# The start of a Fourier-mixing and dense-layer kernel: last filter product through SBUF, tables moved between engines, one set of PSUM pools, and stage 1 of the next batch a slot earlier

## Chip, cores, metric

One core of one Trainium2 chip. The metric is the device time of one execution in microseconds (us), all data in device memory at the start. Lower is better. The kernel is already tuned; its matrix engine has work 99% of the time.

## The reference

```python
X = np.fft.rfft(x, axis=1)                      # x: (8, 3008, 256)
y = np.fft.irfft(X * (filt_r + 1j*filt_i), n=3008, axis=1)
h = y.reshape(24064, 256) @ w_in                # 256 x 2048
g = 0.5 * h * (1 + erf(h / sqrt(2)))            # exact GELU
out = g @ w_out                                 # 2048 x 256, float32
```

## The kernel before

The transform of 3008 points is split as 47 x 64 and done with matmuls in four stages, each against a table of sines. Stage 2's result is multiplied by the filter F on VectorE. Batch 0 is transformed alone at the start, because the dense layers need it, and its intermediate results are turned with TensorE transposes. Batches 1 to 7 are transformed in between the dense matmuls, one piece per *slot*; a slot is one step of 128 hidden columns (`mm1`, 2 matmuls) and, from slot 16 on, one step of the second layer (`mm2`, 4 matmuls). Their intermediate results pass through DRAM (R1, R2). Matmuls write to PSUM, in *banks*; an *eviction* copies a bank to SBUF, the core's on-chip memory. `a_sb` holds the result of stage 1, `vt_sb` that of batch 0's third stage, `d_sb` its transposes and `y_sb` the finished transform. Warm-up matmuls are matmuls on a tile of ones whose result nobody reads.

The last product of batch 0 and its third stage:

```python
def c2(self, p):                       # stage 2 and filter product of batch 0
    w = self.st[0, "p", p] = self.pp.tile([128, 2, 512], BF16, tag="p12", name="p12")
    ps = self.bank("ps_c2", "w")
    ...                                # two matmuls into ps
    if p < 11:
        nc.vector.tensor_tensor(out=w, in0=ps..., in1=f..., op=ALU.mult)
        return
    w, ps = w.rearrange("p t (a b) -> p t a b", a=2), ps.rearrange("p (a b) -> p a b", a=2)
    for c in (slice(0, 128), slice(128, 256)):      # the last one in two pieces
        nc.vector.tensor_tensor(out=w[:, :, :, c], in0=ps[:, :, c]..., in1=f[:, :, :, c], op=ALU.mult)

# main program: products two ahead of the third stage, with warm-up matmuls between
for q in range(1, 7):
    ...
    if q < 6:
        m.c3(2 * q - 2)
        if q == 3:
            m.table_3(2)
            m.table_3_copy(2, True)
        else:
            m.warm_up(1)
    else:
        m.c3(10, 1)
        m.warm_up(1)
        m.c3(11, 1)
m.warm_up(2)
```

The last stages of batch 0, the change of PSUM pools, and the slots of batch 1:

```python
m.psum(wide, v=(4, 1), t=(4, 1))
for u in range(10):
    if u < 8:
        m.c3t(u)                                    # transposes, then d_sb by VectorE
    if u >= 2:
        m.c4(u - 2, (act, False if u > 7 else act)) # stage 4, then y_sb
wide.close()                                        # pools v and t end here
m.psum(ctx, h=(3, 1), o=(2, 1), f=(3, 1))           # pools of the dense layers
...
if b == 1:
    s1, n1, r1, s2, n2, r2, s4, n4 = 1, 4, 16, 26, 2.8, 61, 68, 0.72
```

So batch 1 has stage 1 in slots 1, 5, 9, 13, stage 2 from slot 26, stage 4 from slot 68.

```python
self.pa = pool("pa", 3)                             # three buffers of a_sb
...
def s1(self, b, c):                                 # c = 0..3
    a = self.pa.tile([128, 2, 4, 256], BF16, tag="a", name="a_sb")
    ps = [[self.bank("ps_s1", "h" if i == h == 0 else "f") for h in range(2)] for i in range(2)]
    ...                                             # 8 matmuls
    ...                                             # four evictions on VectorE, ps -> a
    for r in range(2):
        for h in range(2):
            nc.sync.dma_start(out=o[:, w:w + 4, :], in_=a[64 * r:64 * r + 48, h])   # R1 in DRAM
```

Stage 1 takes 8 matmuls and four evictions on VectorE in a slot; its four PSUM banks are one of three of `h`, shared with the dense layers, and all three of `f`. And there are four tiles of `a_sb` but only three buffers.

Of the kernel before, what the change touches and what calls it, by code (L numbers as in the profile page):

```python
# [29 lines left out]
class _Mix:  # L30
# [63 lines left out]
    def dup_filters(self, eng, k0, k):  # L94
        for k in range(k0, k0 + k, 2):
            o, i = (self.F[r:r + 64, :, k:k + 2, :].rearrange("p t a b -> p t (a b)") for r in (64, 0))
            eng.tensor_copy(out=o, in_=i)  # L97

# [26 lines left out]
    def table_1(self, g):  # L125

        nc, ts = self.nc, self.nc.vector.tensor_scalar
        col = lambda name: g.tile([128, 1], FP32, name=name)
        off = g.tile([128, 2, K1], FP32, name="off")
        nc.vector.memset(off[:, 0, :], 0.25)  # L130
        nc.vector.memset(off[:, 1, :], 0.5)
        h, n1, hs, hc = col("h"), col("n1"), col("hs"), col("hc")
        ts(out=h, in0=self.p, scalar1=float(NA), scalar2=None, op0=ALU.is_ge)
        nc.vector.scalar_tensor_tensor(out=n1, in0=h, scalar=-float(NA), in1=self.p, op0=ALU.mult, op1=ALU.add)
        ts(out=hs, in0=h, scalar1=2.0 * PI, scalar2=None, op0=ALU.mult)
        ts(out=n1, in0=n1, scalar1=1.0 / NA, scalar2=None, op0=ALU.mult)
        ts(out=hc, in0=h, scalar1=-2.0 * PI, scalar2=2.0 * PI, op0=ALU.mult, op1=ALU.add)
        self.turn_signs(g)
        self.weights_4(g)
        w, r = g.tile([128, 2, K1], FP32, name="w1"), g.tile([128, 2, K1], FP32, name="r1")  # L140
        nc.vector.scalar_tensor_tensor(out=w, in0=self.k48, scalar=n1, in1=off, op0=ALU.mult, op1=ALU.add)
        ts(out=r, in0=w, scalar1=RND, scalar2=-RND, op0=ALU.add, op1=ALU.add)
        nc.vector.tensor_tensor(out=w, in0=w, in1=r, op=ALU.subtract)
        for q, s in enumerate((hc, hs)):
            nc.scalar.activation(out=self.T1[:, 48 * q:48 * q + 48], in_=w[0:2 * NA].rearrange("p a b -> p (a b)"),
                                 func=AF.Sin, scale=s[0:2 * NA])
# [16 lines left out]
    def table_2_angle(self, g, h):  # L163


        v = self.nc.vector
        ts = v.tensor_scalar
        w = self.gen[:, 0]
        if h == 0:
            col = lambda name: g.tile([128, 1], FP32, name=name)  # L170
            jn = g.tile([128, NB], FP32, name="jn")
            ts(out=jn, in0=self.jj, scalar1=self.n2, scalar2=self.ri, op0=ALU.mult, op1=ALU.add)
            n6, self.n12 = col("n6"), col("n12")
            ts(out=n6, in0=self.n2, scalar1=6.0, scalar2=None, op0=ALU.mult)
            ts(out=self.n12, in0=self.n2, scalar1=12.0, scalar2=None, op0=ALU.mult)
            v.scalar_tensor_tensor(out=w[:, 0:6], in0=self.kk.unsqueeze(2).to_broadcast([128, 6, NB]), scalar=self.n2,
                                   in1=jn.unsqueeze(1).to_broadcast([128, 6, NB]), op0=ALU.mult, op1=ALU.add)
            ts(out=w[:, 6:12], in0=w[:, 0:6], scalar1=n6, scalar2=None, op0=ALU.add)
        else:
            ts(out=w[:, 12:24], in0=w[:, 0:12], scalar1=self.n12, scalar2=None, op0=ALU.add)  # L180
        k = slice(12 * h, 12 * h + 12)
        ts(out=self.gen[:, 1, k].bitcast(I32), in0=w[:, k].bitcast(I32), scalar1=15, scalar2=None,
           op0=ALU.logical_shift_left)

    def turn_signs(self, g):

        ts = self.nc.vector.tensor_scalar
        q, b = (g.tile([128, 1], FP32, name=n) for n in ("q64", "b32"))
        self.turn = [g.tile([128, 1], FP32, name=n) for n in ("turn_r", "turn_i")]
        ts(out=q, in0=self.p, scalar1=64.0, scalar2=-64.0, op0=ALU.is_ge, op1=ALU.mult)  # L190
        self.nc.vector.tensor_tensor(out=q, in0=self.p, in1=q, op=ALU.add)
        ts(out=b, in0=q, scalar1=32.0, scalar2=2.0, op0=ALU.is_ge, op1=ALU.mult)
        ts(out=self.turn[0], in0=b, scalar1=1.0, scalar2=-1.0, op0=ALU.mult, op1=ALU.add)
        ts(out=self.turn[1], in0=b, scalar1=-1.0, scalar2=1.0, op0=ALU.mult, op1=ALU.add)

# [23 lines left out]

    def weights_4(self, g):  # L220

        ts = self.nc.vector.tensor_scalar
        q, self.wt, self.wtc = (g.tile([128, 1], FP32, name=n) for n in ("q48", "wt", "wtc"))
        ts(out=q, in0=self.p, scalar1=48.0, scalar2=-48.0, op0=ALU.is_ge, op1=ALU.mult)
        self.nc.vector.tensor_tensor(out=q, in0=self.p, in1=q, op=ALU.add)
        ts(out=self.wt, in0=q, scalar1=2.0, scalar2=1.0, op0=ALU.is_ge, op1=ALU.add)
        ts(out=self.wtc, in0=self.p, scalar1=4.0, scalar2=1.0, op0=ALU.is_ge, op1=ALU.add)


# [13 lines left out]

    def table_3_copy(self, q, turn):

        v = self.t3.rearrange("p (k n r) -> p k r n", k=8, r=2)
        self._evac(self.T3[:, 8 * q:8 * q + 8], v, "act")
        if turn:
            for r in range(2):
                self._evac(self.T3i[:, 8 * q:8 * q + 8, r, :], v[:, :, 1 - r, :], "act", self.turn[r])  # L250

    def table_3_turn(self, q):

        k = slice(8 * q, 8 * q + 8)
        for r in range(2):
            self.nc.vector.tensor_scalar(out=self.T3i[:, k, r, :], in0=self.T3[:, k, 1 - r, :],
                                         scalar1=self.turn[r], scalar2=None, op0=ALU.mult)

# [142 lines left out]
    def c2(self, p):  # L401
# [9 lines left out]
        if p < 11:  # L411
            nc.vector.tensor_tensor(out=w, in0=ps.unsqueeze(1).to_broadcast([128, 2, 512]),
                                    in1=f.rearrange("p t a b -> p t (a b)"), op=ALU.mult)
            return
        w, ps = w.rearrange("p t (a b) -> p t a b", a=2), ps.rearrange("p (a b) -> p a b", a=2)
        for c in (slice(0, 128), slice(128, 256)):
# [3 lines left out]
    def c3(self, p, np=2):  # L420
# [11 lines left out]
        for half in range(2):  # L432
            v = self.vt[:, half, 0:96, :].rearrange("c a b -> c (a b)").rearrange("c (n k) -> c n k", n=HB)
            self._evac(v[:, :, 8 * p:8 * p + 8 * np], ps[half][:, 0:256 * np].rearrange("c (k n) -> c n k", n=HB),
                       False if p == 11 and half else "act")

    def c3t(self, u):
# [3 lines left out]
        d = self.st[0, "d", u // 2]  # L441
        ps = self.bank("ps_c3t", "t", BF16)
        for i in (0, 2, 4, 6, 1, 3, 5, 7):
# [6 lines left out]
    def c4(self, u, eng):  # L450
# [5 lines left out]
        for half in range(2):  # L456
            ps = self.bank("ps_c4", "v")
            for i in range(4):
# [69 lines left out]
def kernel(  # L528
# [25 lines left out]
    for sgn, lo, base in ((1, 0, 0), (-1, 32, m.S - NA)):  # L554
# [6 lines left out]
    nc.vector.memset(m.ones, 1.0)  # L561
    m.warm_up(10)
    m.table_1(g)
    m.table_2_rows(g)
    m.T1c = g.tile([2 * NA, 96], BF16, name="T1c")
    nc.vector.tensor_copy(out=m.T1c.rearrange("p (k h r) -> p k h r", h=2, r=2),
                          in_=m.T1.rearrange("p (h r k) -> p k h r", h=2, r=2))
    m.gen = m.py.tile([128, 2, K1, NB], FP32, tag="y", name="gen")
    m.table_2_angle(g, 0)
    m.unit_matrices(g, cols)  # L570
    m.T3i = m.pg.tile([128, K1, 2, NB], BF16, tag="g", name="T3i")
    m.vt = m.pg.tile([128, 2, 97, 32], BF16, tag="g", name="vt_sb")
    for k, n in ((0, 4), (4, 8), (12, 12)):
# [8 lines left out]
    for u in range(16):  # L582
# [7 lines left out]
        if u == 7:  # L590
            m.table_2_sin(1)
            m.table_3(0)
            m.table_3_copy(0, False)
            m.warm_up(2)
        if u == 11:
            m.table_2_swap(1)
            m.table_4(m.T4c, m.T1q, m.wtc, "n", False)
            m.table_3_turn(0)
            m.warm_up(1)
    m.table_3(1)  # L600
    m.table_3_copy(1, False)
    m.dup_filters(nc.vector, 0, 4)
    m.warm_up(1)
    m.c1t(0, (False, False))
    m.c1t(1, (act,))
    m.c2(0)
    m.table_3_turn(1)
    m.warm_up(1)
    m.c2(1)
    m.c1t(2, (act,))  # L610
    m.warm_up(2)
    for q in range(1, 7):
        if q < 6:
            m.c2(2 * q)
            if q + 2 < 6:
                m.c1t(q + 2, (act,))
            if q != 3:
                m.warm_up(2)
            m.c2(2 * q + 1)
        if q < 6:  # L620
            m.c3(2 * q - 2)
            if q == 3:
                m.table_3(2)
                m.table_3_copy(2, True)
            else:
                m.warm_up(1)
        else:
# [8 lines left out]
    m.load_w_out(0)  # L636
    m.load_w_out(8)

    warm = g.tile([128, 1], FP32, name="warm")
    nc.scalar.activation(out=warm, in_=m.p, func=AF.Gelu)  # L640
    wide.close()
    wide = ctx.enter_context(ExitStack())
    m.psum(wide, v=(4, 1), t=(4, 1))
    for u in range(10):
        if u < 8:
            m.c3t(u)
        if u >= 2:
            m.c4(u - 2, (act, False if u > 7 else act))
    wide.close()
    m.psum(ctx, h=(3, 1), o=(2, 1), f=(3, 1))  # L650

# [9 lines left out]
    for b in range(1, B):  # L661
        hi = first(b)
        if b == 1:
            s1, n1, r1, s2, n2, r2, s4, n4 = 1, 4, 16, 26, 2.8, 61, 68, 0.72
        else:
# [54 lines left out]
```

## Time and profile before

| | before |
|---|---|
| time, median of 6 runs | 772.76 us (772.1 to 775.15) |
| span of the profiled run | 770.6 us |
| TensorE busy | 763.5 us (99%) |
| first transposes of batch 0's third-stage result (`c3t`) | 31.05 us |
| first dense matmul | 38.76 us |
| first matmul of the second dense layer (slot 16) | 49.13 us |

From about 49 us on TensorE has work without gaps, so the time is decided by when that rhythm is reached. The main lines for this are in the prediction below. VectorE's evictions of stage 1 and the dense matmuls (columns of a timeline: start, busy us, engine, line, operation, output <- inputs, shape, count, and in brackets the idle time before and what ended it):

```profile
39.78 4.88 DVE L271 CAST a_sb<-ps_s 128x512 bf16<-128x512 f32 x8 [1.18 <-PE ps_s L296]
44.95 4.88 DVE L271 CAST a_sb<-ps_s 128x512 bf16<-128x512 f32 x8 [0.29 <-PE ps_s L296]
...
47.83 1.47 PE L482 MATMUL ps_h<-y_sb,w_in_sb 128*128 128x512 bf16 x6
49.13 0.60 PE L509 MATMUL ps_o<-w_out_sb,g_sb 128*128 128x256 bf16 x4
```

Sixteen evictions of 0.61 us run in two groups of eight; the only waits are for the matmuls.

### The profile page before, as it was taken

The numbers are of one execution on the slowest core, as the hardware profiler recorded it, in microseconds if no ns is written. First come the engines' busy times: TensorE is split into PE (matmuls) and PEld (weight loads), VectorE is DVE, ScalarE is ACT, GpSimd is POOL, SyncE is SP. The second block draws the span as 40 slices with busy tenths as digits, with TensorE's granted clock in tenths as the row PEclk, the third lists the DMA queues.
The fourth block names the chain that finished last, engine by engine and source line by source line (L and its number), as shares of the span: only waits on it lengthen the run. The fifth ranks groups of instructions, "written<-read, shape, count | busy, mean of one in ns | idle before, by whom it ended". The sixth has DMA issues, their size and how long they took to land.

```text
span 770.6 us, 15044 instructions
## 1 busy us (share of the span) xinstructions
PE 763.5 (99%) x6057; PEld 527.5 (68%) x6057; DVE 398.5 (52%) x737; ACT 566.7 (74%) x977; POOL 62.5 (8%) x154
## 2 busy tenths in 40 slices
PE   8999999999999999999999999999999999999998
PEld 5857666776766766677777777667676777766666
DVE  8957755564545645466463664627646366411011
ACT  6879855897568975699656996579865798666663
POOL 7701100010000200011000110001100000000000
PEclk9999999999999999999999999999999999999999
DMA  9884645366163661636526364345553422410111
GB/s 153 150 197 115 136 125 129 115 138 155 40 173 88 128 158 47 187 79 125 138 58 176 85 133 124 83 151 105 114 137 84 136 83 70 123 42 28 42 42 55
DMA packets 87270, 85.66 MB, mean 111 GB/s; under 512 B 6688, under 2 KB 77472, under 8 KB 87200
## 3 DMA queue, kind: packets, MB, share of 16 engines
q1 hardware_dynamic: 78816, 68.70, 31.3%
q0 software_dynamic: 8384, 16.00, 14.1%
q8 instruction: 47, 0.77, 0.4%
q14 instruction: 23, 0.19, 0.1%
HBM read 54.00 MB, written 46.66 MB: 131 GB/s over the span
## 4 chain that ended last, share of the span: by engine, by line
PE 94%; DMA 3%; POOL 2%; issue 0%; DVE 0%; POOLq 0%; SPq 0%
PE ps_o L509 43%; PE ps_h L482 42%; PE ps_s L369 2%; PE ps_s L344 2%; PE ps_s L319 2%; PE ps_s L296 2%; DMA x_sb<-in_x_dram 2%; POOL x_sb L83 1%; DMA F<-in_filt_i_dram 1%; POOL F L97 1%; DMA d_sb<-R 0%; POOL F L92 0%; PE ps_e L499 0%; POOL T1s L282 0%; DVE ost L522 0%
## 5 line engine op out<-in xcount | busy, mean ns | idle before, releaser
L485 ACT ACTIVATE g_sb<-ps_h 128x512 bf16<-128x512 f32 x752 | 438.0, 597 | 183.4 <-PE ps_h L482 172.6
L509 PE MATMUL ps_o<-w_out_sb,g_sb 128*128 128x256 bf16 x2992 | 447.5, 273 | 0.0
L482 PE MATMUL ps_h<-y_sb,w_in_sb 128*128 128x512 bf16 (+3 forms) x1600 | 445.8, 366 | 0.7 <-DMA x_sb<-in_x_dram 0.7
L509 PEld LDWEIGHTS <-g_sb 128*128 128x128 bf16 x2992 | 283.9, 98 | 134.3 <-issue 9.9
L482 PEld LDWEIGHTS <-w_in_sb 128*128 128x128 bf16 x1600 | 154.7, 98 | 23.7 <-issue 1.1
L515 DVE COPY ost<-ps_o 128x512 f32<-128x512 f32 x93 | 63.8, 686 | 143.5 <-PE ps_o L509 143.4
L327 DVE TENSOR_TENSOR p<-ps_s,F 128x512 bf16<-128x512 f32 x84 | 58.1, 692 | 105.8 <-ACT p L326 89.4
L273 DVE TENSOR_SCALAR y_sb<-ps_s 128x376 bf16<-128x376 f32 x112 | 61.0, 548 | 80.7 <-PE ps_s L369 80.7
L271 DVE CAST a_sb<-ps_s 128x512 bf16<-128x512 f32 x112 | 69.4, 683 | 27.7 <-PE ps_s L296 27.7
L271 DVE CAST v_sb<-ps_s 128x512 bf16<-128x512 f32 x84 | 57.4, 685 | 2.9 <-PE ps_s L344 2.9
L325 ACT ACTIVATE p<-ps_s 64x512 bf16<-64x512 f32 x84 | 49.8, 593 | 2.0
L326 ACT CAST p<-ps_s 64x512 bf16<-64x512 f32 x84 | 48.5, 577 | 1.0
L369 PEld LDWEIGHTS <-d_sb 96*128 96x128 bf16 x448 | 30.7, 97 | 25.6 <-DMA d_sb<-R 0.6
L102 POOL COPY gate<-p 1x1 bf16<-1x1 bf16 x48 | 8.5, 176 | 470.7 <-DVE p L329 470.7
L329 DVE TENSOR_TENSOR p<-p 128x512 bf16<-128x512 bf16 x84 | 35.7, 425 | 2.9
L369 PE MATMUL ps_s<-T,d_sb 96*128 96x94 bf16 x448 | 36.3, 204 | 0.1
L328 DVE TENSOR_TENSOR p<-p,F 128x512 bf16<-128x512 bf16 x84 | 34.9, 415 | 0.0
L83 POOL DMA_DIRECT2D x_sb<-in_x_dram x64 | 32.6, 511 | 13.3 <-issue 12.8
L344 PE MATMUL ps_s<-p,T 128*128 128x256 bf16 x168 | 32.1, 273 | 0.0
L319 PE MATMUL ps_s<-b_sb,T 128*128 128x256 bf16 x168 | 32.1, 273 | 0.0
L344 PEld LDWEIGHTS <-T 128*128 128x128 bf16 x168 | 16.4, 98 | 20.1 <-DVE p L329 0.5
L319 PEld LDWEIGHTS <-T 128*128 128x128 bf16 x168 | 16.4, 98 | 13.4
(113 smaller groups left out, 195.0 us busy)
## 6 DMA issues: line engine op xcount, KB each, us to landing
out_dram<-ost SPq DMA_DIRECT2D x93, 256.0 KB, 2.4
x_sb<-in_x_dram POOLq DMA_DIRECT2D x64, 188.0 KB, 3.6
R<-a_sb SPq DMA_DIRECT2D x112, 96.0 KB, 2.1
b_sb<-R SPq DMA_DIRECT2D x28, 384.0 KB, 4.1
R<-v_sb SPq DMA_DIRECT2D x42, 256.0 KB, 3.3
d_sb<-R SPq DMA_DIRECT2D x56, 192.0 KB, 4.7
w_in_sb<-in_moe_w_in_dram POOLq DMA_DIRECT2D x2, 512.0 KB, 9.0
w_out_sb<-in_moe_w_out_dram POOLq DMA_DIRECT2D x2, 512.0 KB, 11.0
```

What stands on the lines that cost most here:

```text
L271: self.nc.vector.tensor_copy(out=out, in_=in_)
L273: self.nc.vector.tensor_scalar(out=out, in0=in_, scalar1=scale, scalar2=None, op0=ALU.mult)
L319: nc.tensor.matmul(ps[:, 256 * i:256 * i + 256], lhsT=self.T2[:, k].rearrange("p a b -> p (a b)"), rhs=self.st[b, "b", k // 6][:, k % 6, : ...
L325: nc.scalar.activation(out=p2[0:64], in_=ps[64:128], func=AF.Copy, scale=-1.0)
L326: nc.scalar.copy(out=p2[64:128], in_=ps[0:64])
L327: nc.vector.tensor_tensor(out=p1, in0=ps, in1=f(0), op=ALU.mult)
L344: nc.tensor.matmul(ps[:, 256 * i:256 * i + 256], lhsT=self.T3[:, k].rearrange("p a b -> p (a b)"), rhs=w[:, 256 * i:256 * i + 256], start= ...
L369: nc.tensor.matmul(ps[:, 94 * i:94 * i + 94], lhsT=d[:, (grp % 2) * 4 + i, 128 * half:128 * half + 128], rhs=t4, start=True, stop=True)
L482: nc.tensor.matmul(ps[:, o:o + n], lhsT=self.w_in_sb[:, dc, jc * 128:jc * 128 + 128], rhs=self.ring[:, dc, off:off + n], start=(dc == 0), ...
L485: nc.scalar.activation(out=self.st["g", t][:, jc, :], in_=ps, func=AF.Gelu)
L509: nc.tensor.matmul(ps[:, tile_i % 2, :], lhsT=g[:, jc, tile_i * 128:tile_i * 128 + 128], rhs=self.w_out_sb[:, jc, :], start=(jc == 0), sto ...
L515: nc.vector.tensor_copy(out=ost, in_=ps)
```

## The change

It is meant to shorten the start: work moves from VectorE to ScalarE or GpSimd, the last filter product is copied to SBUF first so that VectorE multiplies at the faster rate, the last table's transposes come earlier, and batch 0's last stages use the PSUM pools of the dense layers, so that stage 1 of batch 1 can come in slots 0, 4, 8, 12, ahead of the first dense matmul. The core of the diff (sign tables by memset, reordered angle work and the signature changes that go with them are cut):

```diff
 def dup_filters(self, eng, k0, k):
-            eng.tensor_copy(out=o, in_=i)
+            (eng.copy if eng is self.nc.scalar else eng.tensor_copy)(out=o, in_=i)
 # c2, last product
-        w, ps = w.rearrange("p t (a b) -> p t a b", a=2), ps.rearrange("p (a b) -> p a b", a=2)
+        z = self.z
+        nc.scalar.copy(out=z, in_=ps)
+        w, ps = w.rearrange("p t (a b) -> p t a b", a=2), z.rearrange("p (a b) -> p a b", a=2)
 # c3, evictions of vt
-                       False if p == 11 and half else "act")
+                       False if p >= 10 and half else "act")
 # c3t and c4: banks
-        ps = self.bank("ps_c3t", "t", BF16)
+        ps = self.bank("ps_c3t", "f", BF16)
-            ps = self.bank("ps_c4", "v")
+            ps = self.bank("ps_c4", "h" if (2 * u + half) % 5 < 3 else "o")
 # main program
     m.table_3(1)
-    m.table_3_copy(1, False)
-    m.dup_filters(nc.vector, 0, 4)
+    m.dup_filters(nc.scalar, 0, 2)
+    m.table_3_copy(1)
+    m.dup_filters(nc.vector, 2, 2)
...
     m.c2(0)
-    m.table_3_turn(1)
+    m.table_3_turn(1, 0, False)
...
     m.c1t(2, (act,))
-    m.warm_up(2)
+    m.table_3(2)
+    m.table_3_copy(2)
+    m.warm_up(1)
     for q in range(1, 7):
...
-            if q != 3:
-                m.warm_up(2)
+            m.warm_up(2)
...
             m.c3(2 * q - 2)
-            if q == 3:
-                m.table_3(2)
-                m.table_3_copy(2, True)
-            else:
-                m.warm_up(1)
+            m.warm_up(1)
+            if q < 4:
+                m.table_3_turn(*((1, 1), (2, 0), (2, 1))[q - 1], act)
...
     wide.close()
-    wide = ctx.enter_context(ExitStack())
-    m.psum(wide, v=(4, 1), t=(4, 1))
+    m.psum(ctx, h=(3, 1), o=(2, 1), f=(3, 1))
...
-            m.c4(u - 2, (act, False if u > 7 else act))
-    wide.close()
-    m.psum(ctx, h=(3, 1), o=(2, 1), f=(3, 1))
+            m.c4(u - 2, (False if u > 7 else act, act))
...
-            s1, n1, r1, s2, n2, r2, s4, n4 = 1, 4, 16, 26, 2.8, 61, 68, 0.72
+            s1, n1, r1, s2, n2, r2, s4, n4 = 0, 4, 15, 25, 2.8, 61, 68, 0.72
```

More of the change, by code (lines that the diff above doesn't have):

```diff
@@ L137, in table_1 @@
         ts(out=hc, in0=h, scalar1=-2.0 * PI, scalar2=2.0 * PI, op0=ALU.mult, op1=ALU.add)
-        self.turn_signs(g)
-        self.weights_4(g)
+        self.table_2_rows(g)
         w, r = g.tile([128, 2, K1], FP32, name="w1"), g.tile([128, 2, K1], FP32, name="r1")
@@ L177, in table_2_angle @@
                                    in1=jn.unsqueeze(1).to_broadcast([128, 6, NB]), op0=ALU.mult, op1=ALU.add)
+            self.T1c = g.tile([2 * NA, 96], BF16, name="T1c")
+            v.tensor_copy(out=self.T1c.rearrange("p (k h r) -> p k h r", h=2, r=2),
+                          in_=self.T1.rearrange("p (h r k) -> p k h r", h=2, r=2))
             ts(out=w[:, 6:12], in0=w[:, 0:6], scalar1=n6, scalar2=None, op0=ALU.add)
@@ L183, in table_2_angle, with signs, weights_4 @@
            op0=ALU.logical_shift_left)
-    def turn_signs(self, g):
-        ts = self.nc.vector.tensor_scalar
-        q, b = (g.tile([128, 1], FP32, name=n) for n in ("q64", "b32"))
+    def signs(self, g):
+        set_ = self.nc.vector.memset
         self.turn = [g.tile([128, 1], FP32, name=n) for n in ("turn_r", "turn_i")]
-        ts(out=q, in0=self.p, scalar1=64.0, scalar2=-64.0, op0=ALU.is_ge, op1=ALU.mult)
-        self.nc.vector.tensor_tensor(out=q, in0=self.p, in1=q, op=ALU.add)
-        ts(out=b, in0=q, scalar1=32.0, scalar2=2.0, op0=ALU.is_ge, op1=ALU.mult)
-        ts(out=self.turn[0], in0=b, scalar1=1.0, scalar2=-1.0, op0=ALU.mult, op1=ALU.add)
-        ts(out=self.turn[1], in0=b, scalar1=-1.0, scalar2=1.0, op0=ALU.mult, op1=ALU.add)
+        for t, s in zip(self.turn, (-1.0, 1.0)):
+            set_(t, s)
+            for lo in (32, 96):
+                set_(t[lo:lo + 32], -s)
+        self.wtc = g.tile([128, 1], FP32, name="wtc")
+        set_(self.wtc, 2.0)
+        set_(self.wtc[0:4], 1.0)
+    def weights_4(self, g):
+        ts = self.nc.gpsimd.tensor_scalar
+        q, self.wt = (g.tile([128, 1], FP32, name=n) for n in ("q48", "wt"))
+        ts(out=q, in0=self.p, scalar1=48.0, scalar2=-48.0, op0=ALU.is_ge, op1=ALU.mult)
+        self.nc.gpsimd.tensor_tensor(out=q, in0=self.p, in1=q, op=ALU.add)
+        ts(out=self.wt, in0=q, scalar1=2.0, scalar2=1.0, op0=ALU.is_ge, op1=ALU.add)
     def unit_matrices(self, g, cols):
@@ L218, in table_2_swap @@
                        "act", 1.0 - 2.0 * i)
-    def weights_4(self, g):
-        ts = self.nc.vector.tensor_scalar
-        q, self.wt, self.wtc = (g.tile([128, 1], FP32, name=n) for n in ("q48", "wt", "wtc"))
-        ts(out=q, in0=self.p, scalar1=48.0, scalar2=-48.0, op0=ALU.is_ge, op1=ALU.mult)
-        self.nc.vector.tensor_tensor(out=q, in0=self.p, in1=q, op=ALU.add)
-        ts(out=self.wt, in0=q, scalar1=2.0, scalar2=1.0, op0=ALU.is_ge, op1=ALU.add)
-        ts(out=self.wtc, in0=self.p, scalar1=4.0, scalar2=1.0, op0=ALU.is_ge, op1=ALU.add)
     def table_4(self, t4, t1, wt, tag, eng):
@@ L242, in table_3, with table_3_copy, table_3_turn @@
                                      self.T2[:, 8 * q + i].rearrange("p a b -> p (a b)"), self.eye)
-    def table_3_copy(self, q, turn):
+    def table_3_copy(self, q):
         v = self.t3.rearrange("p (k n r) -> p k r n", k=8, r=2)
         self._evac(self.T3[:, 8 * q:8 * q + 8], v, "act")
-        if turn:
-            for r in range(2):
-                self._evac(self.T3i[:, 8 * q:8 * q + 8, r, :], v[:, :, 1 - r, :], "act", self.turn[r])
-    def table_3_turn(self, q):
+    def table_3_turn(self, q, r, eng):
         k = slice(8 * q, 8 * q + 8)
-        for r in range(2):
-            self.nc.vector.tensor_scalar(out=self.T3i[:, k, r, :], in0=self.T3[:, k, 1 - r, :],
-                                         scalar1=self.turn[r], scalar2=None, op0=ALU.mult)
+        self._evac(self.T3i[:, k, r, :], self.T3[:, k, 1 - r, :], eng, self.turn[r])
     def warm_up(self, n):
@@ L562 @@
     m.warm_up(10)
+    m.signs(g)
     m.table_1(g)
-    m.table_2_rows(g)
-    m.T1c = g.tile([2 * NA, 96], BF16, name="T1c")
-    nc.vector.tensor_copy(out=m.T1c.rearrange("p (k h r) -> p k h r", h=2, r=2),
-                          in_=m.T1.rearrange("p (h r k) -> p k h r", h=2, r=2))
     m.gen = m.py.tile([128, 2, K1, NB], FP32, tag="y", name="gen")
@@ L571 @@
     m.T3i = m.pg.tile([128, K1, 2, NB], BF16, tag="g", name="T3i")
+    m.z = g.tile([128, 512], BF16, name="z")
     m.vt = m.pg.tile([128, 2, 97, 32], BF16, tag="g", name="vt_sb")
@@ L592 @@
             m.table_3(0)
-            m.table_3_copy(0, False)
+            m.table_3_copy(0)
             m.warm_up(2)
@@ L597 @@
             m.table_4(m.T4c, m.T1q, m.wtc, "n", False)
-            m.table_3_turn(0)
+            m.table_3_turn(0, 0, False)
+            m.table_3_turn(0, 1, False)
             m.warm_up(1)
     m.table_3(1)
-    m.table_3_copy(1, False)
-    m.dup_filters(nc.vector, 0, 4)
+    m.dup_filters(nc.scalar, 0, 2)
+    m.table_3_copy(1)
+    m.dup_filters(nc.vector, 2, 2)
     m.warm_up(1)
@@ L637 @@
     m.load_w_out(8)
+    m.weights_4(g)
     warm = g.tile([128, 1], FP32, name="warm")
```

## The prediction

> **What bounds the kernel now.** I read the page first, then busy time by stretch, then the timelines of single engines in the first 50 us, which is where every edited line runs.
>
> ```profile
> span 770.6 us, 15044 instructions
> PE 763.5 (99%) x6057; PEld 527.5 (68%) x6057; DVE 398.5 (52%) x737; ACT 566.7 (74%) x977; POOL 62.5 (8%) x154
> ...
> 14.00:30.00 16.00, 15.15 (x188) 12.19 (x188) 15.83 (x19) 13.27 (x20) 15.27 (x24) 1.00 0.84 140
> 30.00:39.00 9.00, 8.07 (x140) 6.92 (x136) 6.80 (x12) 7.77 (x19) 4.07 (x7) 1.00 1.05 184
> 39.00:49.00 10.00, 9.96 (x64) 3.59 (x63) 8.93 (x15) 7.32 (x15) 0.00 (x0) 1.00 1.04 185
> 49.00:100.00 51.00, 50.92 (x364) 35.17 (x363) 29.10 (x56) 44.43 (x80) 5.52 (x16) 1.00 0.61 144
> 100.00:400.00 300.00, 300.00 (x2375) 207.50 (x2376) 165.16 (x298) 219.92 (x377) 16.36 (x48) 1.00 0.47 117
> ```
>
> The columns of the stretches are length, then TensorE, weight loads, VectorE, ScalarE, GpSimd (busy us, count). From 49 us on TensorE has no gap (300.00 of 300). What happens there is the dense layers and batches 1 to 7, and it takes what its matmuls take. So the change can only move the moment at which the dense layers reach their full rhythm, and whatever it saves before 49 us arrives one for one at the end. In 14 to 30 us TensorE's busy figure includes warm-up matmuls; VectorE is the full engine (15.83 of 16).
>
> ```profile
> 13.99 0.90 DVE L97 COPY F<-F 64x1024 bf16<-64x1024 bf16 x2
> 14.92 0.76 DVE L271 COPY b_sb<-ps_c1t 128x512 bf16<-128x512 bf16 x2
> 15.82 1.23 DVE L412 TENSOR_TENSOR p<-ps_c,F 128x1024 bf16<-128x1024 f32 x1
> 16.96 0.35 DVE L256 TENSOR_SCALAR T3i<-T,turn_r 128x512 bf16<-128x512 bf16 x1
> 17.22 0.35 DVE L256 TENSOR_SCALAR T3i<-T,turn_i 128x512 bf16<-128x512 bf16 x1
> 17.41 2.04 POOL L97 COPY F<-F 64x1024 bf16<-64x1024 bf16 x2 [0.55 <-DMA F<-in_filt_i_dram]
> 17.48 2.35 DVE L412 TENSOR_TENSOR p<-ps_c,F 128x1024 bf16<-128x1024 f32 x2
> ...
> 28.80 1.28 DVE L417 TENSOR_TENSOR p<-ps_c,F 128x512 bf16<-128x512 f32 x2
> 30.57 0.42 DVE L271 CAST vt_sb<-ps_c 128x256 bf16<-128x256 f32 x1 [0.49 <-PE ps_c L430]
> 31.75 5.56 DVE L271 COPY d_sb<-ps_c3t 96x1024 bf16<-96x1024 bf16 x8 [0.75 <-PE ps_c3t L445]
> 37.28 0.55 DVE L273 TENSOR_SCALAR y_sb<-ps_c 128x376 bf16<-128x376 f32 x1
> 38.06 0.55 DVE L273 TENSOR_SCALAR y_sb<-ps_c 128x376 bf16<-128x376 f32 x1 [0.22 <-PE ps_c L459]
> ```
>
> Read this as one chain: filter products (L412, a start every 1.132 us), the split last product (L417), the last eviction of vt, eight evictions of d, the last y. With TensorE after it:
>
> ```profile
> 36.41 1.60 PE L459 MATMUL ps_c<-T4c,d_sb 96*128 96x94 bf16 x24
> 38.76 0.59 PE L482 MATMUL ps_h<-y_sb,w_in_sb 128*128 128x512 bf16 x2 [0.73 <-DMA x_sb<-in_x_dram]
> 39.28 0.63 PE L296 MATMUL ps_s<-x_sb,T1s 47*64 47x512 bf16 x8
> ...
> 41.66 1.06 PE L296 MATMUL ps_s<-x_sb,T1s 47*64 47x512 bf16 x8
> ...
> 46.88 1.01 PE L296 MATMUL ps_s<-x_sb,T1s 47*64 47x512 bf16 x8
> ```
>
> TensorE idles 0.73 us before the first dense matmul. The row blames a load of x, but that matmul reads y and w_in, and in the instruction order it waits on VectorE, ScalarE and the semaphores of the w_in loads, which x uses again. VectorE's last y ends at 38.06+0.55 = 38.61; that is the true release. Note the two L296 groups of 1.06 and 1.01 against 0.63: there stage 1 of batch 1 waits for its PSUM banks, which VectorE empties.
>
> **What the Trainium skill says.** "VectorE: DVE Perf Modes", section "The perf-mode tier table": a tensor_tensor in bf16 from SBUF runs at two elements a cycle, with any operand in PSUM at one. The trace agrees: the product of batches 1 to 7 takes 692 ns with PSUM in (L327) and 415 ns all in SBUF (L328), both 128x512; L417 takes 683. "GPSIMD Engine Reference", section "1. Specifications": GpSimd shares its SBUF interfaces with VectorE and contends with instructions of two SBUF inputs. Before, GpSimd's ten copies of F run beside products with one operand in PSUM and keep 1033 to 1054 ns, so no contention shows; the rewritten product has two SBUF inputs, but comes after the copies end at 27.31. "TensorE: Matmul & The Clock Gate", section "Back-to-back issue gap": about N/2.4 + 2.5 ns, so 216 ns for 512 columns. The chain of waits has 0.43 us for the two matmuls of a dense slot and 0.44 for four of 256 columns: the dense part is at that floor, nothing is left to win there.
>
> **The change part by part.**
>
> 1. Front end (sign tables by memset, angle work reordered). First-stage TensorE work begins at 5.92, 8.64, 10.60 and 12.48 us; the landing records of the pairs of x loads end within 0.14 us of each. The loads are not touched: I count 0.
>
> 2. VectorE loses before its second product one copy of F (0.45, half of the 0.90 for two) and one turn of T3 (0.26, from 16.96 to 17.22). That is 0.71. But product number 2 needs F's upper half, which GpSimd's first copy writes: 17.41 + 1.03 = 18.44, and that copy waits for a load. Product 2 started at 17.48 + 1.13 = 18.61; it can now start at about 18.50. Of 0.71 only **0.1** is left. ScalarE takes over the copy and the turns, some 1.0 + 3 x 0.55 us, minus two turns it already did; my list of its work in order shows each piece done 1 us or more before its reader.
>
> 3. Last product by way of SBUF: two pieces at 415 instead of 683 ns, 0.54 less on VectorE. The extra ScalarE copy of 128x512 (about 0.56, as evictions of vt) starts when the last forward matmuls are done, about 28.1, and ends about 28.7, just as product 10 ends; it costs at most 0.05. VectorE is then done at 29.5 instead of 30.08. But the vt evictions on ScalarE before the transposes (five in 1.92 us from 28.89, ending 30.81) start only when the third stage's matmuls of products 8 and 9 are done, and these move with part 2 only. One of the five moves to VectorE (-0.25). ScalarE ends at about 30.5, so the transposes start near 30.65 instead of 31.05: **0.4** for parts 2 and 3 together.
>
> 4. Last table's transposes ahead, two more warm-ups on TensorE. In the product stage TensorE needs about 2.4 us per pair of products against VectorE's 2.26 in three of the rounds, with about 0.5 us of lead. I count 0.
>
> 5. Last stages on the dense layers' pools. The d evictions stay eight at 0.695 us and set the pace: 0 inside. At the end the first half of the last y goes to VectorE and the second to ScalarE. The half that is ready first is now VectorE's, so it need not wait from 37.83 to 38.06; the last y ends about **0.1** earlier relative to d.
>
> 6. Stage 1 of batch 1 moves from slot 1 to slot 0, ahead of the first dense matmul, and needs no y. Its eight matmuls (0.56 us in the chain) fit into the hole of 0.73 us while the last y is evicted. Its first two loads had landed by 32.8 us. That hides **0.55**.
>
> 7. VectorE begins emptying stage 1's banks right after its last y, relative to the first dense matmul about 1.2 us sooner (39.78 - 38.76 = 1.02 after it before, 0.2 ahead of it now). The two stalls (1.06 - 0.63 and 1.01 - 0.63, 0.8 us in sum) shrink; following four evictions of 0.61 us against four dense slots of 0.46 I get about 0.35 left: **0.45**.
>
> 8. Stage 2 of batch 1 one slot earlier (25 for 26). Its b loads follow the stage-1 writes, which move by about 2 us; stage 2 would start 0.87 + 1.5 = 2.4 us earlier, and b's first load had 1.4 us to spare (landed 56.6, used 58.02). Enough left: 0.
>
> Sum: 0.4 + 0.1 + 0.55 + 0.45 = **1.5 us**. 772.7 - 1.5 = 771.2 us, 0.2%.
>
> **Rivals.**
> - *Everything removed from VectorE counts*: 0.71 + 0.54 + 0.25, plus parts 5 to 7, 2.6 us, 770.1. Against it: GpSimd's copy at 18.44 and ScalarE's vt evictions at the end. For it: those two limits rest on tenths of a microsecond.
> - *ScalarE takes over as the bound*: it gets the copy of F at 14 us, ahead of T3 and b evictions; if b for product 2 came 1 us later than I have it (16.9), or the SBUF copy fell behind an eviction, VectorE would wait and parts 2 and 3 turn to 0 or -0.5. Then only parts 5 to 7 stay: 771.7 to 772.2.
> - *A transfer takes back the gain later*: b or w_out landing after its now earlier use. w_out's landings end at 42.7 and 45.3, first use would be near 47.7; slack 2 us, but stage 1's writes now overlap that load. Worth up to +0.8 us: 772.
>
> **Range and chances.** The shortest executions before lay at 772.1 and 772.7, one at 775.15, so the median itself is good to about 0.5. With the rivals at 770.1 and 772.2, I take 771.2, from 769.9 to 772.4. Two per cent is 15 us; everything before the dense layers lasts 38.76 us and most of it is loads and work that stay. Faster by over 2%: 0.01, slower: 0.005, within: 0.985.
>
> **What would show it.** Part 1: first-stage matmuls at the same four times. Part 2: VectorE idle about half a microsecond before product 2, which starts near 18.5 on GpSimd's copy. Part 3: last product pieces near 415 ns; transposes of vt released by ScalarE near 30.6. Part 5: last y near 38.1. Part 6: L295 matmuls ahead of the first dense one, whose idle time falls under 0.2. Part 7: repeated stage-1 groups nearer 0.8. First output matmul at 47.6 instead of 49.13. From there on both traces should run the same with a fixed offset; an idle time of TensorE after 50 us that before has not would make the prediction wrong, as would a first dense matmul later than 38.5.

## The result

The changed kernel took **773.65 us** in the median of six runs (771.72 to 775.88), against 772.76 of the kernel before. The ratio is 1.0011, 95% interval 0.9986 to 1.0035: the same time. Here and below a ratio is the mean time of one kernel's fast runs over that of the other's of the same rounds, so it is not quite the ratio of the medians quoted. The gain of 1.5 us did not come, and 773.65 lies above the range of 769.9 to 772.4.

The page of the changed kernel's profiled run (774.64 us):

```profile
span 772.9 us, 15051 instructions
PE 764.0 (99%) x6059; PEld 527.7 (68%) x6059; DVE 397.3 (51%) x735; ACT 568.6 (74%) x979; POOL 63.8 (8%) x157
```

VectorE has 1.2 us less to do, and the span is 2.3 us longer. Where the time goes is in the chain that ended last (start, us, what):

```profile
38.26 2.46 DVE a_sb L270 x4
40.74 5.82 DMA R<-a_sb
46.62 1.52 DMA R<-a_sb
48.14 0.70 DVE a_sb L270
48.88 1.86 PE ps_h L484 x4
```

In the kernel before, this chain is TensorE alone from 38.76 us on. Now it leads from stage 1's first tile through two waits for its writes to DRAM (5.82 and 1.52 us) back into VectorE and only then to TensorE. The same in the timelines of VectorE and TensorE:

```profile
18.37 4.62 DVE L411 TENSOR_TENSOR p<-ps_c,F 128x1024 bf16<-128x1024 f32 x4 [0.41 <-POOL F L97]
23.24 5.75 DVE L411 TENSOR_TENSOR p<-ps_c,F 128x1024 bf16<-128x1024 f32 x5 [0.25 <-POOL F L97]
29.00 0.76 DVE L419 TENSOR_TENSOR p<-z,F 128x512 bf16<-128x512 bf16 x2
...
43.39 2.48 DVE L270 CAST a_sb<-ps_s 128x512 bf16<-128x512 f32 x4 [0.29 <-PE ps_s L295]
48.13 2.48 DVE L270 CAST a_sb<-ps_s 128x512 bf16<-128x512 f32 x4 [2.26 <-DMA R<-a_sb]
```

```profile
37.77 0.63 PE L295 MATMUL ps_s<-x_sb,T1s 47*64 47x512 bf16 x8
38.33 1.90 PE L484 MATMUL ps_h<-y_sb,w_in_sb 128*128 128x512 bf16 x8
...
46.27 1.04 PE L484 MATMUL ps_h<-y_sb,w_in_sb 128*128 128x512 bf16 x4
48.88 1.86 PE L484 MATMUL ps_h<-y_sb,w_in_sb 128*128 128x512 bf16 x4 [1.58 <-DVE a_sb L270]
50.54 1.06 PE L511 MATMUL ps_o<-w_out_sb,g_sb 128*128 128x256 bf16 x4
```

Read them together. The x8 group of evictions before 49 us of the old kernel has split into x4 and x4, with 2.26 us between them in which VectorE waits for a DMA: the fourth `a_sb` tile needs the first tile's buffer, and that is still being written out. Meanwhile stage 1's fourth group keeps its bank of `h`; slots 12 and 13 fill the other two banks, and slot 14 finds none. TensorE, which had reached slot 13 at about 46.7 us (46.27 + 0.43) against 47.83 before, 1.1 us ahead, stands still and reaches slot 16 at 50.54 against 49.13, 1.4 us behind.

Why are the writes late? They are issued 1.55 us earlier (first issue 40.15 us, before 41.70), but their landings are no earlier. Issue to landing, in the same view as above:

```profile
DMA to landing us min/median/max: 1.9/4.3/6.4
```

The four writes of the first tile land at 45.74, 46.56, 47.26 and 48.02 us, before at 45.36 to 46.23. The DMA queues' packets and shares in 43 to 44 us say why, in the kernel before and then in the changed one (q0 carries the loads that GpSimd issues, here x of batch 1 and `w_out`; q1 carries the writes of R1):

```profile
q0 software_dynamic: 200, 0.10, 72.9%
q1 hardware_dynamic: 279, 0.13, 51.5%
```

```profile
q0 software_dynamic: 347, 0.18, 130.5%
q1 hardware_dynamic: 58, 0.03, 10.5%
```

While the loads have packets, the writes get few: in the changed kernel 1 packet from 42 to 43 us and 58 in the next, in both kernels none before 42. In these traces the writes move only as the load queue drains, and here it drains later: it moved 213 packets in 44 to 45 us against 50 before, 46 against none in 46 to 47. Part of this is a later start: GpSimd issues `w_out` at 33.05 us (33.01 in a second trace) against 32.23, because its copies of F waited once more for a filter load (0.88 and 1.14 us). Variants of the kernel before, below, show the same wait (0.43 and 0.90 us) and issue `w_out` at 33.24 and 33.55, so nothing ties this part to the change.

There is a second effect in this trace. After the stand-still TensorE's clock was halved for about 3.4 us (stretch 48.9 to 52.3 us; the third number from the right, ahead of DMA share and GB/s, is the granted clock):

```profile
48.90:52.30 3.40, 3.40 (x11) 1.47 (x11) 1.72 (x3) 1.20 (x2) 0.00 (x0) 0.51 0.62 145
```

By estimate that costs half of 3.4, 1.7 us. Of the first six runs, three show a mean clock of 0.997 to 0.998 and took 774.64, 775.58 and 775.88 us; the other three at clock 1.0 took 771.72 to 772.67; these were not profiled, so how long they stood still is not known. (One run of the kernel before took 775.15; its clock was not recorded.) Whether the halving or the wait is the cause is a question for the experiments.

### The profile page after: what moved, and what is told of

The parts are those of the page before. It is cut to its first block, busy times and chain, and to the rows that moved or that the text cites. A ratio compares the mean times of both kernels' runs of the same rounds, so it can differ in the third digit from the quotient of the medians.

```text
span 772.9 us, 15051 instructions
## 1 busy us (share of the span) xinstructions
PE 764.0 (99%) x6059; PEld 527.7 (68%) x6059; DVE 397.3 (51%) x735; ACT 568.6 (74%) x979; POOL 63.8 (8%) x157
## 4 chain that ended last, share of the span: by engine, by line
PE 95%; DMA 2%; DVE 1%; POOL 1%; issue 0%; POOLq 0%; DVEq 0%; SPq 0%
PE ps_o L511 43%; PE ps_h L484 41%; PE ps_s L368 2%; PE ps_s L343 2%; PE ps_s L318 2%; PE ps_s L295 2%; DMA R<-a_sb 1%; DMA x_sb<-in_x_dram 1%; DMA F<-in_filt_i_dram 1%; PE ps_c L432 1%; PE ps_c3t L447 0%; POOL x_sb L83 0%; DVE a_sb L270 0%; DVE p L411 0%; PE ps_c L407 0%; PE ps_warm L262 0%
## 6 DMA issues: line engine op xcount, KB each, us to landing
w_out_sb<-in_moe_w_out_dram POOLq DMA_DIRECT2D x2, 512.0 KB, 12.9
```

## The experiments

Theory A: the earlier stage 1 collides with the loads, its writes land late, the three `a_sb` buffers run out, and the stand-still of TensorE takes back the gain. Theory B: nothing systematic is lost; the gain is really too small to see, and the slow runs with the halved clock make the median. The first four kernels ran on one chip (kernel before there: median 772.66 of 9 runs, 772.09 to 773.78), the last four on another (773.09 of 9, 772.76 to 773.29). Five runs each.

One quantity takes out the chance of when the first loads land: the time from the first `c3t` transposes to slot 16. I give it with each kernel, after the time. It still contains the end of the load queue that the writes wait for.

**The changed kernel again.** No edit.

> The changed kernel once more, beside its variants on one chip. Both theories: median 772 to 775.5 us. Theory A (stage 1 of batch 1 now runs while the output weights still load; its fourth tile waits for its buffer until the first tile's writes have landed; VectorE and then TensorE stand still, and after the stand-still the clock is halved for one window): the wait of VectorE on the writes of a_sb is 1 to 2.5 us in the profile, and runs with a granted clock under 1.000 are 2 to 4 us longer than those at 1.000. Theory B (the slow runs are the chip's noise and have nothing to do with that wait): the same spread in the variants of this call that have no such wait.

Measured: 773.15 us (772.42 to 773.56), ratio 1.0005 (0.9992 to 1.0017). The clock was 1.0 in four runs and 0.999 in one. The wait is there and longer, VectorE first and TensorE after it:

```profile
48.59 2.48 DVE L270 CAST a_sb<-ps_s 128x512 bf16<-128x512 f32 x4 [2.75 <-DMA R<-a_sb]
...
49.34 1.02 PE L484 MATMUL ps_h<-y_sb,w_in_sb 128*128 128x512 bf16 x4 [2.07 <-DVE a_sb L270]
```

Slot 16 comes at 50.20 us. The wait is longer than the 1 to 2.5 us expected, and the run at 0.999 (773.26) is not the slowest. So the halving is no constant companion of the stand-still, as the expectation had it, and in this series the kernel without it is still not faster. The stand-still alone takes the gain here.

**A fourth buffer.** A fourth buffer of `a_sb` does not fit in SBUF, but the pool of `d_sb` is free at that time and has the size.

```diff
-        a = self.pa.tile([128, 2, 4, 256], BF16, tag="a", name="a_sb")
+        pool, tag = (self.pd, "d") if (b, c) == (1, 3) else (self.pa, "a")
+        a = pool.tile([128, 2, 4, 256], BF16, tag=tag, name="a_sb")
```

> The changed kernel, with only the fourth stage-1 tile of batch 1 in a buffer of the d tiles, idle then. Theory A: no wait of VectorE on the writes, no idle time of TensorE over 0.3 us after the first dense matmul, granted clock 1.000 in every run, 770.9 to 771.5 us, that is 1.3 to 1.9 us under the kernel before. Theory B: 772 to 775.5 us as the changed kernel, with runs at a clock under 1.000 as often as there. A third (C): the output weights land too late for the second layer itself; then TensorE waits at the third output slot instead, 771.5 to 773 us.

Measured: 771.48 us (771.29 to 771.75), ratio 0.9984 (0.9971 to 0.9996), 1.67 us under the same kernel without the buffer on the same chip, and 1.18 under the kernel before, a little less than the 1.3 to 1.9 expected. The wait is gone although the writes are as late as ever (median 4.6 us to landing):

```profile
44.00 4.87 DVE L270 CAST a_sb<-ps_s 128x512 bf16<-128x512 f32 x8 [0.29 <-PE ps_s L296]
...
48.61 0.60 PE L512 MATMUL ps_o<-w_out_sb,g_sb 128*128 128x256 bf16 x4
```

From `c3t` to slot 16 it takes 16.98 us, against 18.08 in the kernel before and 19.21 in the changed kernel of the run above. Theory A holds, but for its halved clock, and B falls: the writes land as late as before, only what waits for them changed, and the time came back. No run of the one kernel overlaps one of the other.

**The weights early.** The other end of the collision: `w_out` is loaded right after `w_in`, so that the load queue is empty when the writes come.

```diff
     m.load_w_in()
+    m.load_w_out(0)
+    m.load_w_out(8)
...
     m.load_x(1)
-    m.load_w_out(0)
-    m.load_w_out(8)
```

> The changed kernel, with the two loads of the output weights issued right after those of the input weights, 17 us earlier, so that they have landed before stage 1 writes; still three buffers. Theory A: the writes of the first tile land within 2.5 us of their issue instead of 5 to 8, the fourth tile finds its buffer free, granted clock 1.000, 770.9 to 771.5 us. If the writes are slow for another reason than the weights: the wait stays at 1 us or more and the time at 772 or more.

Measured: 772.04 us (771.89 to 772.67), ratio 0.9992 (0.998 to 1.0005). The writes now land after 2.2 us in the median, the first tile's by 45.09, and neither VectorE nor TensorE waits there: 16.97 us from `c3t` to slot 16, the same as with the buffer. But GpSimd needs 1.8 us to issue the two loads, and its copies of F come that much later (18.89 us; 17.30 in the changed kernel), with the products behind them:

```profile
19.96 10.28 DVE L411 TENSOR_TENSOR p<-ps_c,F 128x1024 bf16<-128x1024 f32 x9 [0.93 <-POOL F L97]
```

`c3t` starts at 32.27 us instead of 30.99. The cause is confirmed from its other side, but the cure costs over half of what it brings: 1.28 us of the 2.24 that it saves after `c3t`. So the 770.9 to 771.5 us expected were missed.

**The slot back.** Stage 1 of batch 1 in slots 1, 5, 9, 13 as before, all else changed.

```diff
-            s1, n1, r1, s2, n2, r2, s4, n4 = 0, 4, 15, 25, 2.8, 61, 68, 0.72
+            s1, n1, r1, s2, n2, r2, s4, n4 = 1, 4, 15, 25, 2.8, 61, 68, 0.72
```

> The changed kernel, with only stage 1 of batch 1 back in slot 1 (its b loads and stage 2 stay a slot early). By the prediction's parts 6 and 7 alone this would cost 0.5 to 0.6 us. Theory A: stage 1 is 0.4 to 0.5 us later relative to the dense matmuls, but the writes are still behind the output weights, so the wait of the fourth tile shrinks by about 0.5 us only and is still over 0.5 us; 772 to 774.5 us. If slot 0 alone made the trouble: no wait, 771.5 to 772 us.

Measured: 772.27 us (772.18 to 773.25), ratio 0.9998 (0.9984 to 1.0011); 18.21 us from `c3t` to slot 16. A shorter wait remains (1.02 us on VectorE, 0.34 on TensorE), and the idle time before the first dense matmul is back at 0.57 us.

The tile asks for the buffer 1.2 us later than in the first trace of the changed kernel (47.11 against 45.87) and gets it at the same 48.13 (48.59 in the repeated run). That agrees with a release set by the load queue, not by stage 1.

**Without two late warm-ups.** With the fourth buffer, and without the warm-up matmul after the third stage of products 8 and 9 and the one between the last two.

```diff
             m.c3(2 * q - 2)
-            m.warm_up(1)
+            if q < 5:
+                m.warm_up(1)
...
             m.c3(10, 1)
-            m.warm_up(1)
             m.c3(11, 1)
```

> The kernel with the fourth buffer, less two warm-up matmuls: the one behind the third stage of products 8 and 9, and the one between the third stages of products 10 and 11. Theory D (why the prediction's part 3 brought nothing: from the last forward matmuls to the end of the third stage TensorE works without a gap, 2.43 us of which 0.44 are these two, so a faster last product has nothing to shorten): the transposes of vt start 0.2 to 0.3 us earlier, 0.2 us under the fourth-buffer kernel, that is 771.0 to 771.5 us. Rival (ScalarE's four evictions of vt are the bound, or the clock drops without the warm-ups): no change or slower.

Measured: 771.03 us (770.76 to 772.35), ratio 0.9976 (0.9964 to 0.9989), the fastest of all. The stage after the last product is what it aims at. From its last stage-2 matmuls (L408) to the transposes (L448) it takes 2.82 us:

```profile
28.08 0.38 PE L408 MATMUL ps_c<-b_sb,T 128*128 128x256 bf16 x2
...
30.90 1.50 PE L448 MATMUL ps_c3t<-eye,vt_sb 128*128 128x128 bf16 x24
```

In the changed kernel repeated it is 3.11 (27.88 to 30.99), in the kernel before 3.25 (27.80 to 31.05). So this stretch was TensorE's, and the two warm-ups of 0.22 us each were part of it; of their 0.43 us, 0.29 arrived. The granted clock stayed at 0.999 to 1.0 without them. Its ratio interval and that of the fourth buffer alone overlap, so the trace shows this gain and the time does not prove it.

**The last product from PSUM.** With the fourth buffer, but the detour by way of SBUF undone.

```diff
-        z = self.z
-        nc.scalar.copy(out=z, in_=ps)
-        w, ps = w.rearrange("p t (a b) -> p t a b", a=2), z.rearrange("p (a b) -> p a b", a=2)
+        w, ps = w.rearrange("p t (a b) -> p t a b", a=2), ps.rearrange("p (a b) -> p a b", a=2)
```

> The kernel with the fourth buffer, with the last product taken from PSUM again, no copy on ScalarE. The prediction's part 3 expects 0.3 us more. Theory D: the last product then ends at the same distance from the last forward matmuls as in the kernel before, TensorE waits 0.1 us more: 0.05 to 0.15 us over the fourth-buffer kernel, which the timing will hardly show; in the profile two pieces of 683 ns and the gap of TensorE before the last four third-stage matmuls.

Measured: 771.37 us (770.81 to 771.82), ratio 0.9978 (0.9966 to 0.9991): as fast as the versions with the detour, within what the runs resolve. From the last stage-2 matmuls to the transposes it takes 3.24 us against 3.11 with it. The product by way of SBUF is worth 0.13 us, though VectorE's two pieces fell from 1.28 to 0.76.

**Slot 0 alone, in the kernel before.**

```diff
-            s1, n1, r1, s2, n2, r2, s4, n4 = 1, 4, 16, 26, 2.8, 61, 68, 0.72
+            s1, n1, r1, s2, n2, r2, s4, n4 = 0, 4, 16, 26, 2.8, 61, 68, 0.72
```

> The kernel before, with only stage 1 of batch 1 moved to slot 0, three buffers. Parts 6 and 7 of the prediction: 1.0 us less, 771.7. Theory A: most of that, as the weights are issued 0.8 us earlier here than in the changed kernel, but the fourth tile may wait up to 1 us on the first tile's writes: 771.7 to 772.5 us.

Measured: 773.03 us (772.37 to 773.89), ratio 0.9999 (0.9985 to 1.0013); 18.17 us from `c3t` to slot 16. Two waits take the place of the old one:

```profile
39.33 0.63 PE L296 MATMUL ps_s<-x_sb,T1s 47*64 47x512 bf16 x8 [0.69 <-ACT y_sb L269]
...
48.22 2.48 DVE L271 CAST a_sb<-ps_s 128x512 bf16<-128x512 f32 x4 [0.75 <-DMA R<-a_sb]
```

With separate pools stage 1 may not start until the last y has left the old banks, so the hole of 0.7 us stays open: the earlier slot needs the shared pools. And the wait for the buffer appears here too. The 771.7 to 772.5 us expected were missed, since the hole was not counted.

**The fourth buffer alone, in the kernel before.** Same edit as above.

> The kernel before with only the fourth stage-1 tile of batch 1 in a buffer of the d tiles. Control: there the writes of the first tile have landed 0.9 us before the fourth tile is evicted, so no theory expects a change: 772.3 to 773 us. It also shows the first 39 us of the kernel before on this chip. If the plain kernel before has such waits in its longer runs (772.8 to 773.8), this one has none of them and a spread as narrow as the fourth-buffer kernel's, 0.5 us.

Measured: 772.82 us (772.28 to 773.45), ratio 0.9998 (0.9985 to 1.001); 18.09 us from `c3t` to slot 16 against 18.08. The buffer is worth nothing where nothing waits for its release (a margin of 1.2 us in the first trace; in this one the first tile's writes land by 47.20 us, 0.6 before the fourth tile starts). The five runs spread over 1.2 us, nine of the plain kernel before on that chip over 0.5, so nothing here puts its longer runs down to such waits. The buffer's gain in the changed kernel is therefore the removal of a wait which the change made.

## Why the prediction was wrong

The step that failed is the rival "a transfer takes back the gain": it put the cost at no more than 0.8 us, for `b` or `w_out`, and did not count any wait for stage 1's own writes. The runs show VectorE waiting 2.26 and 2.75 us for these writes; that is 2.2 us of the time to slot 16, more than the 1.5 us forecast. The cause is settled by the pair with and without the buffer, on the same chip, and by its control in the old kernel. Against the prediction's own steps:

| step | predicted | shown |
|---|---|---|
| 2 and 3: transposes sooner | 0.4 | 0.03 to 0.06 in the two traces of the changed kernel |
| 5, 6 and 7: last y, hole, bank stalls | 1.1 | 1.10 once nothing waits for the writes (18.08 to 16.98) |
| 8: stage 2 a slot earlier | 0 | likely 0.2 to 0.4, not isolated |
| a transfer takes back the gain | up to -0.8, as a rival | -2.2 (19.21 to 16.98), more with the halved clock |

**Rival "a transfer takes back the gain": the step that failed.** It said that "stage 1's writes now overlap that load", and then asked only whether `b` or `w_out` would land after its use. It did not ask who waits for the writes themselves. The bookkeeping it lacked was short: four tiles, three buffers, so tile 4 waits for tile 1's landing; that had a margin of 1.2 us; moving stage 1 forward by about 1.5 us without moving the load queue's end spends it. This alone would have given only about 0.4 us. The rest, up to the 2.26 and 2.75 measured, is that the writes land 1.8 and 2.3 us later. Of this the later issue of the loads can explain 0.8. For what is left, the loads of `w_out` themselves take longer in the changed kernel: 12.9 and 13.5 us to landing in the two traces of the changed kernel, against 11.0 in the kernel before and in its version with the buffer. Why they do I can't say from the runs.

**Part 7** counted the PSUM banks as stage 1's only limit. In addition its own size was wrong: the two stalled groups stayed at 1.01 and 1.00 us (1.06 and 1.01 before) instead of falling near 0.8. The part measured VectorE's start against the first dense matmul, but the next group of stage 1 comes a slot earlier too: from the first eviction to that group it is 1.88 us before (39.78 to 41.66) and 1.93 in the changed kernel (38.23 to 40.16). That parts 5 to 7 still sum to 1.1 is luck: two errors cancel. Up to the end of slot 0, with tile 1 done, the changed kernel with the buffer gains 1.02 us (8.79 us after `c3t` before, 7.77 in it, taking slot 0 as 0.46 us), where parts 5 and 6 promised 0.65; part 7 gives the remaining 0.08 instead of 0.45.

**Part 6** was right in its mechanism: stage 1 starts at 37.77 us, the first dense matmul follows at 38.33 without idle time (38.76 with 0.73 before). The run of slot 0 alone shows that this needs part 5's pools.

**Part 3** was the second failed term. VectorE's saving of 0.5 us came as computed, but the prediction took the vt evictions to be free to move with it. TensorE had no gap there: from the last stage-2 matmuls to the transposes it ran the third stage and warm-ups for 3.11 us, and the SBUF detour only removed 0.13 of waiting. "TensorE needs about 2.4 us per pair of products against VectorE's 2.26" stood in part 4; it was not applied to the last pair.

**Part 2** was right where it looked: product 2 started at 18.37 us after 0.41 us of waiting for GpSimd's copy of F (predicted 18.50 and half a microsecond). But it did not follow F further. VectorE waited for the next filter load too, 0.25 us before product 6 (0.51 in the repeated run; none in the trace of the kernel before, 0.24 in its variant with slot 0), and the last stage-2 matmuls came at 27.91 and 27.88 us against 27.80. So the 0.1 was lost again. **Part 5**: the last y ends 1.1 us after the last d, before 1.3; predicted 0.1 better, shown 0.2. **Parts 1 and 4** at 0: no run contradicts them.

**Part 8** was counted as 0. From slot 16 to the end the kernel before and its two variants need 721.4 to 721.5 us, but the six traces with stage 2 in slot 25 and full clock need 721.1 to 721.2. Part of it is visible: weight loads of stage 4 of batch 1 wait 0.57 us for `d_sb` in the kernel before, 0.38 to 0.40 in its two variants, and 0 to 0.19 in these. In the changed kernel's first trace, which fell behind by the halved clock, it is 0.48. No run moved this slot alone, so I take it as likely, not as proven.

Together, for the changed kernel repeated: -0.06 - 1.10 - 0.42 + 2.23 = +0.65 us of span, which is what the traces show (771.29 against 770.64). With the buffer the kernel takes 771.48 us, close to the 771.2 predicted, but that too is partly luck: the 0.4 us of parts 2 and 3 did not come, and part 8's gain, counted as 0, stands in for it. For the first trace the halved clock comes on top.

Of the prediction's own tests the first output matmul decided: it was to come at 47.6 us and came at 50.54. The one stated as proof of error, idle time after 50 us, looked just behind the place; the hole lies at 47.1 to 48.9.

**The best version.** The changed kernel with the fourth buffer and without the two late warm-ups takes 771.03 us, 0.24% under the kernel before on the same chip, interval 0.11 to 0.36%.

## What to carry to other kernels

When a step is moved earlier, list everything it holds until its results are out, SBUF buffers as well as PSUM banks, and for each the margin between its release and the next use; here the buffer released by a DMA did not move with the compute (its writes were issued 1.55 us earlier and landed no earlier). In the chain of waits before a change, a margin like the 1.2 us here is invisible, because nothing waits there yet. And a saving on one engine counts only if the engine it feeds has an idle gap at that place: look for the gap first.

## What the Trainium skill lacked or had wrong

- "TensorE: Matmul & The Clock Gate", section "What's actually happening", puts the fall to half clock after at least one idle window of about 3.4 us. Here a hole of 1.75 us (46.27 + 0.86 for four matmuls, to 48.88; the profile, with modelled ends, says 1.58) was followed by a granted clock of 0.51 over the 3.4 us from 48.9 to 52.3, and a hole of 2.25 us in the repeated run (47.09 to 49.34) was not: 1.00 from 48 to 53. The length of the slow phase agrees. What the section lacks is that half clock can follow a single hole about half as long as the window; that the hole set it off is likely, not shown.
- "DMA: Bandwidth & Descriptors", section "Queues, rings and completion order", says that each engine goes round the queue rows with work, a packet at a time. Here the write queue, with writes issued from 40.15 us, moved 1 packet in 42 to 43 us and 58 in the next, beside 374 and 347 of the load queue, and the time from issue to landing rose from 2.4 to 4.3 us in the median. An even share could not be counted on; the runs don't show why. It need not contradict the page: the profile's packets carry about 0.5 KB here (0.18 MB in 347), and the page's packet joins several descriptors. What the page lacks is how long one queue can hold the engines.
- "Perfetto Trace Analysis", section "Optimization Strategy", takes a repeating gap as the sign of too few buffers. Here a single gap (2.26 us on VectorE, once) was that sign, and cost more than the change gained.
